# Attention's product buffers, the early parts and the wo blocks of a gated scan kernel: four moves in the order of work

## The chip, the cores and the metric

The kernel runs on one core of one Trainium2 chip. The metric is the device time of one execution in microseconds (us). Before the change it is 760.67 us, the median of three runs (758.78 to 761.59).

Engines are named as in the profile: PE is TensorE, DVE VectorE, ACT ScalarE, POOL GpSimd, SP SyncE. SP computes nothing here and issues most of the DMA transfers, one behind the other. Each engine works through its own instructions in the order of the program and waits for other engines through semaphores.

## The reference

`x` is 2048 rows of 640 numbers. It is normalised by rows (`xn`), goes through attention and through a gated layer, and the two are multiplied:

```
xn = layernorm(x)
s  = attention(xn @ wqkv) @ wo        # 32 heads of 20; each row looks at 8 earlier rows, two apart
g  = silu(((xn @ w_gate) * (xn @ w_up)) @ w_down)
out = x + s * g
```

All arrays are float32.

## The kernel before

**Numbers in two parts.** The matmuls take their operands as float32r. The kernel splits every operand in a high part (a copy in that type, made by ACT) and a low part (the rest, a subtraction by DVE or POOL), and each product is three products: high by high, high by low, low by high. `split` (line 107) and `mm3` (line 114) do this.

**Rows.** The 2048 rows are 16 tiles of 128, four to a chunk. Tile 0 to 7 are the even rows, 8 to 15 the odd ones. Tiles come in by DMA, `moments_q` (320) takes mean and variance on DVE, `scales` (327) makes the factors from them: a square root on ACT, a sum and a reciprocal on DVE, and for tiles 8 to 15 the rest, seven small steps, on POOL. `spread` (337) brings the factors to all partitions with one small matmul and an ACT copy, `apply_q` (349) applies them on ACT, `trans_q` (359) turns a tile on DVE and splits it. The result is `xT`, four chunks.

**Products with fewer multiplications.** The gate and up products, the product with w_down and the one with wo are done as a seven product scheme on two by two blocks (Strassen's), which needs sums and differences of blocks of both operands. For chunks 0 and 1 those of `xT` are made early: `early_sums(k)` (583), eight additions and subtractions on POOL, and `early_high(k)` (596), which splits four results on POOL and stores the eight parts with eight DMAs on SP, to `t_scr` and `e_scr`. k is 0 or 1. The results live in the memory of two earlier tiles, `xc` (tag "kv") and `xe` (tag "t"). For chunks 2 and 3 the same is done later by `differences` (1187) on ACT and POOL.

**Buffers.** Memory is handed out by tags: `st(shape, "t", 2)` is one of two buffers of the tag "t". A tile gets a buffer that is free once everything that used it before is done; the waits follow from that. At the start the two "t" buffers are `xa` (at the end tiles 12 to 14) and `xe`. `attention` takes both: `twice` (line 466) for the products of queries and keys, and `terms` (467) for those of weights and values. After attention the "t" buffers take the rows of wo. The tag "gh" has five buffers for pieces of the gate and up results.

**Order of work.** The order is written out by hand, and `attention` is a generator that the rest drives: `advance(budget)` (608) lets it issue instructions worth so much time after each piece of PE work. Attention works in 12 units of four or six heads. In each unit DVE does a product of queries and keys (line 527) and its sum (534) for each pair of the eight positions; a unit later DVE forms weights times values (498), and POOL (in the last unit partly DVE) adds them up (504). The keys and values of a unit come back from DRAM, where `qkv` (420) has stored them by a DMA on ACT's queue (445).

The start of the program, around the change (lines 1105 to 1160), goes: qkv of tiles 4 and 5, three steps of `early_sums(0)`, `scales(8)`, the other five steps, qkv of tiles 6 and 7, moments of tiles 12 to 15, `scales(12)`, `early_high(0)`, `early_sums(1)`, `early_high(1)`, `gate_up(0, 1)` with `spread(8)` in its middle, trans_q of tiles 8 to 10, `gate_up(1, 1)` with `spread(12)` in its middle, qkv of tiles 8 to 11, `gate_up(0, 2)`, the last trans_q, and then attention begins beside qkv of tiles 12 to 15. `gate_up(f, ch)` (627) is one block of gate and up columns for one chunk. Its last multiplication (653) and the store of h (657) are put off to the next `finish_piece()`.

**The groups.** From block f = 2 on, `group(f, c0)` (1284) does a block of columns for two chunks in seven products, at the steps n = 0 to 6. The middle blocks (3 to 10) are done for chunks 2 and 3 (`second` = 0) and then for chunks 0 and 1 (`second` = 1). `hold` (1292) has ACT copy a product into a gh buffer, `gate_a` (1305), `gate_b` (1295), `up_a` (1308) add or multiply on DVE, `up_b` (1298) and `h_b` (1301) on POOL or DVE. up_a and h_b are followed by stores of h (1281) and are put off to step 0 of the next group. The dictionary `beside` hangs further work on a step: the key (f, second, n) is the place. f0 is 10, f1 is 11, the last block.

**The product with wo.** `load_wo` (685) loads rows of wo, `split_wo` (692) splits one, `sums_wo` (930) forms four differences on DVE (936 to 939). `load_pair(p)` (967) loads two tiles of attention's result, `turn_pair(p)` (976) turns them on DVE and forms their sums, `begin_last` (1430) finishes attention and issues the loads of wo. Before the change these hang on the steps as follows:

```
beside.update({(f0, 1, 0): lambda: begin_last(), (f0, 1, 4): lambda: split_wo(0, nc.vector),
               (f0, 1, 5): lambda: split_wo(1, nc.vector), (f0, 1, 6): lambda: sums_wo()})
```

Inside `begin_last`, `load_pair(0)` follows the loads of wo. `load_pair(1)` hangs on (f1, 0, 0) and `turn_pair(0)` on (f1, 0, 1).

Later come the product with wo in pairs of tiles, and the product with w_down with the gate and the sum with x, which fill PE to the end.

Of the kernel before, what the change touches and what calls it, by code (L numbers as in the profile page):

```python
# [19 lines left out]
P = 128  # L20
# [4 lines left out]
NE = NT // DIL  # L25
# [9 lines left out]
CMAX = max(GROUPS) * DH  # L35
# [21 lines left out]
def kernel(  # L57
# [11 lines left out]
    nc = tc.nc  # L69
# [11 lines left out]
    def st(shape, tag, bufs, dt=F32):  # L81
        cnt[0] += 1
        return sb.tile(shape, dt, tag=tag, bufs=bufs, name=f"{tag}_{cnt[0]}")
# [214 lines left out]
    def low_parts(n=None):  # L298
        for _ in range(len(halves) if n is None else n):
            halves.pop(0)()  # L300
# [23 lines left out]
    def load_xq(s, n, t):  # L324
        nc.sync.dma_start(t, xq[:, s - TPC:s - TPC + n, :])

    def scales(s0):
        mv, mr = stat[s0]
        eng = nc.vector if s0 == TPC else nc.gpsimd
        rstd(mv[:, :, 1], mr[:, 1, :], TPC, eng=eng)  # L330
        eng.tensor_scalar(mr[:, 0, :], mv[:, :, 0], -1.0, None, op0=ALU.mult)
        eng.tensor_mul(mr[:, 0, :], mr[:, 0, :], mr[:, 1, :])
        own[s0] = part(few[:, s0 // TPC % 2 * 32:], [P, NQ, 2, TPC])
        eng.tensor_mul(own[s0], mr.unsqueeze(1).to_broadcast([P, NQ, 2, TPC]),
                             quarter.unsqueeze(2).unsqueeze(3).to_broadcast([P, NQ, 2, TPC]))

    def spread(s0):

        p = pt([P, NQ, 2, TPC], "q", 3)
        nc.tensor.matmul(p, sel, own[s0], start=True, stop=True)  # L340
        spread_t[s0] = part(few[:, 64 + s0 // TPC % 2 * 32:], [P, NQ, 2, TPC])
        nc.scalar.activation(spread_t[s0], p, AF.Copy)
        apply_q(s0)
# [117 lines left out]
    def attention():  # L461

        def flat(y):
            return y.rearrange("p i c -> p (i c)")

        twice = st([P, 2, NE * CMAX], "t", 2)
        terms = st([P, 2, NE * CMAX], "t", 2)
        spots = NE * W
        m_ps = weights[0:1, CH - spots:].rearrange("p (i w) -> p i w", w=W)
        nc.vector.tensor_copy(m_ps, mask)  # L470
# [125 lines left out]
    def early_high(k):  # L596

        r0, r1, a, b = early_t[:4]
        for n, (j, y) in enumerate((("T1", a), ("T2", b), ("T3", r0), ("T4", r1))):
            hi = early_t[4 + n].bitcast(F32R)  # L600
            nc.gpsimd.tensor_copy(hi, y)
            nc.gpsimd.tensor_sub(y.bitcast(F32R), y, hi.bitcast(F32))
            for l, t in enumerate((early_t[4 + n], y)):
                nc.sync.dma_start(t_scr[:, T2_UNIT[j, l] + k] if j != "T4" else e_scr[l][:, k], t)
# [22 lines left out]
    def gate_up(f, ch, between=(), amid=(), part=None, early=()):  # L627
        if part is None:
            pp = [pt([P, CH], "g", 2), pt([P, CH], "u", 2)]
            c = slice(0, CH)  # L630
        else:
            pp, c = part, slice(CH // 2, CH)
        last = (f, ch) == (KF - 1, NCH - 1)
        if early:
            gate_up_half(f, ch, 0, pp[0], c, parts=ALL3[:1], last=False)
            for act in early:
                act()
        gate_up_half(f, ch, 0, pp[0], c, parts=ALL3[1:] if early else ALL3, first=not early)
        for act in amid:
            act()  # L640
        gs = st([P, CH], "gh", 5)
        nc.scalar.activation(gs, pp[0], AF.Copy)
        for act in between:
            act()
        share = (c.stop - c.start) / CH
        finish_piece()
        advance(PACE * 3.25 * share)
        gate_up_half(f, ch, 1, pp[1], c)

        def finish():  # L650
            hs = st([P, CH], "gh", 5)
            if not last:
                nc.vector.tensor_mul(hs, pp[1], gs)
            else:
                nc.scalar.activation(hs, pp[1], AF.Copy)
                nc.gpsimd.tensor_mul(hs, hs, gs)
            nc.sync.dma_start(h_scr[ch * TPC:(ch + 1) * TPC, :, f, :].rearrange("t p c -> p t c"),
                              hs.rearrange("p (t c) -> p t c", c=P))

        unfinished.append(finish)  # L660
        if last:
            finish_piece()
        advance(PACE * 3.25 * share)
# [28 lines left out]
    def split_wo(k, eng=nc.gpsimd):  # L692
        y = slot([P, 2, D])
        hi, lo = y[:, 0], y[:, 1]
        split(eng, wo_raw.pop(k), hi, lo)
        wo_s[k] = hi, lo
# [233 lines left out]
    def sums_wo():  # L930

        r, u = wo_keep[:2]
        b11, b12, b21, b22 = r[:, :, :HALF], r[:, :, HALF:], u[:, :, :HALF], u[:, :, HALF:]
        t1, t2, t3 = (wo_sum[0][:, 2 * i:2 * i + 2] for i in range(3))
        t4 = st([P, KS, HALF], "o", 1)
        nc.vector.tensor_sub(t1, b12, b11)
        nc.vector.tensor_sub(t3, b22, b12)
        nc.vector.tensor_sub(t2, b22, t1)
        nc.vector.tensor_sub(t4, b21, t2)
        wo_keep.append({"T1": t1, "T3": t3, "T2": t2, "T4": t4})  # L940
# [26 lines left out]
    def load_pair(p):  # L967
        t = slot([P, 2, D], F32) if p == 2 else st([P, 2 if p else 5, D], "t" if p else "kv", 2)
        if not p:
            wo_sum.append(t[:, 2:].rearrange("p a (b c) -> p (a b) c", c=HALF))  # L970
            t = t[:, :2]
        load_o(2 * p, 2, t)
        t = t.rearrange("p a c -> p (a c)")
        pair_raw[p] = t[:, :3 * KS * P].rearrange("p (a c) -> p a c", c=P)
# [35 lines left out]
    def lo_pair(p, part):  # L1010
        z, raw = pair_z[p, part]
        nc.vector.tensor_sub(z[1], raw, z[0].bitcast(F32))
# [94 lines left out]
    early = early_sums(0)  # L1107
# [4 lines left out]
    load_xq(8, 2, xp)  # L1112
    load_xq(10, 2, xs)
    scales(8)
    for _ in early:
        pass
    qkv(0, 0, 6)
    qkv(0, 0, 7)
    moments_q(12, 4)
    load_xq(12, 3, xa)  # L1120
    load_xq(15, 1, xd)
    scales(12)
    early_high(0)
    for _ in early_sums(1):
        pass
    early_high(1)
    gate_up(0, 1, amid=(lambda: spread(8),))
    nc.scalar.activation(st([P, 1], "exp", 1), eps_t, AF.Exp)
    trans_q(8)
    trans_q(9)  # L1130
# [15 lines left out]
    gate_up(0, 2)  # L1146
    trans_q(15)
    low_parts()
    for a in range(2):
        nc.sync.dma_start(e_scr[2 + a], xT[3][a][:, 0:2, :].bitcast(F32))  # L1150
    made.add(0)
# [9 lines left out]
    f0, f1 = KF - 2, KF - 1  # L1161
# [234 lines left out]
    for m, t in ((m, t) for m in range(1, len(MADE)) for t in range(DIL)):  # L1396
# [23 lines left out]
        elif (m, r) == (last, 1):  # L1420
            for k in range(2):
# [2 lines left out]
    w_split(2, "R")  # L1424
    w_sum.pop(2)
    load_wf(3)
    beside.update({(f0, 1, 0): lambda: begin_last(), (f0, 1, 4): lambda: split_wo(0, nc.vector),
                   (f0, 1, 5): lambda: split_wo(1, nc.vector), (f0, 1, 6): lambda: sums_wo()})

    def begin_last():  # L1430
        advance(1e9)
        wo_keep.extend([load_wo((0, 1)), load_wo((2, 3)), load_wo((4,))[:, 0]])
        load_pair(0)
        begin_wd("T4")

    wo_keep = []
# [15 lines left out]
    for f in range(2, f1):  # L1452
# [18 lines left out]
        if f == F_TWO:  # L1471
# [1 line left out]
        group(f, 2)  # L1473
        group(f, 0, 1)
    places.clear()
    beside.update({(f1, 0, 0): lambda: load_pair(1), (f1, 0, 1): lambda: turn_pair(0), (f1, 0, 4): lambda: (hi_pair(0, 0), lo_pair(0, 0)),
                   (f1, 0, 6): lambda: (hi_pair(0, 1), lo_pair(0, 1), load_e(3, 1, 3)), (f1, 0, 5): sum_w5,
                   (f1, 0, 3): lambda: load_e(3, 0, 2)})
    group(f1)
# [192 lines left out]
```

## Time and profile before

| | |
|---|---|
| runs | 760.67 us median (758.78 to 761.59) |
| the profiled execution | 757.63 us |
| its span in the trace | 755.9 us |
| PE busy | 740.4 us (98%) |
| DVE busy | 612.5 us (81%) |
| POOL busy | 464.2 us (61%) |
| ACT busy | 301.4 us (40%) |
| DMA | 132.98 MB, 176 GB/s on average |

A row of the timeline gives the start in us from the span's start, the duration, the engine, the line of the kernel, the operation, what it writes and reads by the program's names, the shapes, and how many like it are merged in the row. In brackets stands how long the engine was idle ahead of it, and who ended that idle time. A row of waits gives the waiting engine with its tile and line, the one waited for, and then the sum in us, how many times, and the longest. "SPq" and "ACTq" mark the issue of a DMA. PEld is the loading of weights into PE. In a table by stages each row has the stretch, the busy time of PE, PEld, DVE, ACT and POOL, the granted PE clock as a share of full speed, the share of DMA, and GB/s.

### The profile page before, as it was taken

How to read it: one execution, taken by the hardware profiler on the slowest of the kernel's cores; microseconds unless marked ns; L12 is line 12 of the kernel's file. 1: busy time of each engine (PE TensorE's matmuls, PEld its weight loads, DVE VectorE, ACT ScalarE, POOL GpSimd, SP SyncE). 2: the span in 40 equal slices, each digit the busy share in tenths (PEclk: the TensorE clock that was granted, in tenths of full speed). 3: DMA queues.
4: the chain of work that ended last, by engine and by line, in shares of the span. 5: the costliest groups of instructions: out<-in, count | busy, mean ns of one | idle time of the engine just before them, and what ended most of it. 6: DMA issues, size and time to landing. Idle time of an engine off the chain costs nothing. (4 is left out here: it accounts for less than half of the span.)

```text
span 755.9 us, 11101 instructions
## 1 busy us (share of the span) xinstructions
PE 740.4 (98%) x4054; PEld 673.8 (89%) x4054; DVE 612.5 (81%) x720; ACT 301.4 (40%) x577; POOL 464.2 (61%) x389
## 2 busy tenths in 40 slices
PE   8999999899999999999999999998999999999997
PEld 6988879888899998888887888886999999999997
DVE  7666499599978778999899899667898787777775
ACT  5648222323233233233233323333465664444442
POOL 6169636978789779978888989876749900000000
PEclk9999999999999999999999999999999999999999
DMA  8464583586454638776246433366568565555534
GB/s 326 155 194 156 175 278 121 174 264 193 137 170 143 204 131 262 219 204 208 89 123 169 117 90 87 94 176 178 154 178 239 190 254 189 188 188 189 189 105 140
DMA packets 103493, 132.98 MB, mean 176 GB/s; under 512 B 22696, under 2 KB 74404, under 8 KB 103438
## 3 DMA queue, kind: packets, MB, share of 16 engines
q1 hardware_dynamic: 84686, 112.77, 48.0%
q10 hardware_dynamic: 17600, 14.26, 5.8%
q0 software_dynamic: 1152, 5.24, 2.1%
q8 instruction: 32, 0.52, 0.3%
q14 instruction: 23, 0.19, 0.1%
HBM read 83.58 MB, written 47.81 MB: 174 GB/s over the span
## 5 line engine op out<-in xcount | busy, mean ns | idle before, releaser
L504 POOL TENSOR_TENSOR o<-o,t 128x960 f32<-128x960 f32 (+1 forms) x69 | 139.7, 2025 | 19.1 <-DVE t L498 17.6
L498 DVE TENSOR_TENSOR t<-e,kv 128x960 f32<-128x960 f32 (+1 forms) x96 | 99.4, 1037 | 22.1 <-POOL o L504 22.0
L527 DVE TENSOR_TENSOR t<-q,kv 128x1920 f32<-128x1920 f32 (+1 forms) x48 | 92.4, 1925 | 11.4 <-DMA e_scr<-t 8.0
L534 DVE TENSOR_REDUCE lg<-t 128x96 f32<-128x1920 f32 (+1 forms) x48 | 92.2, 1921 | 0.1
L428 PE MATMUL q<-s,xc 128*128 128x360 f32 (+1 forms) x450 | 85.3, 340 | 2.7 <-ACT s L441 2.0
L110 POOL TENSOR_TENSOR s<-wraw,s 128x384 fp32r<-128x384 f32 (+6 forms) x58 | 70.1, 1219 | 28.8 <-ACT s L109 27.0
L428 PEld LDWEIGHTS q<-s,xc 128*128 128x128 f32 x450 | 76.9, 191 | 7.0 <-ACT s L441 2.3
L1292 ACT ACTIVATE gh<-g 128x512 f32<-128x512 f32 x54 | 32.3, 598 | 117.9 <-PE g L1325 105.0
L428 PE MATMUL u<-s,xc 128*128 128x360 f32 (+1 forms) x360 | 66.6, 336 | 0.0
L428 PEld LDWEIGHTS u<-s,xc 128*128 128x128 f32 x360 | 61.0, 188 | 2.3
L428 PE MATMUL g<-s,xc 128*128 128x360 f32 (+1 forms) x330 | 62.3, 340 | 0.0
L428 PEld LDWEIGHTS g<-s,xc 128*128 128x128 f32 x330 | 56.6, 188 | 2.6
L896 PE MATMUL q<-xc,s 128*128 128x320 f32 x342 | 55.5, 309 | 0.0
L1325 PE MATMUL u<-xc,s 128*128 128x512 f32 x216 | 55.1, 390 | 0.0
L1325 PE MATMUL g<-s,s 128*128 128x512 f32 x216 | 54.8, 389 | 0.0
L896 PEld LDWEIGHTS q<-xc,s 128*128 128x128 f32 x342 | 51.5, 188 | 0.0
L1325 PEld LDWEIGHTS u<-xc,s 128*128 128x128 f32 x216 | 40.4, 188 | 8.9 <-ACT gh L1292 0.6
L1325 PEld LDWEIGHTS g<-s,s 128*128 128x128 f32 x216 | 40.5, 188 | 8.4
L109 ACT ACTIVATE s<-wraw 128x384 fp32r<-128x384 f32 (+6 forms) x59 | 33.5, 587 | 29.9 <-PE g L1325 9.4
L504 POOL TENSOR_TENSOR o<-t 128x960 f32<-128x960 f32 (+1 forms) x12 | 24.4, 2033 | 34.0 <-DVE t L498 24.9
L1325 PE MATMUL g<-xc,s 128*128 128x512 f32 x168 | 42.3, 396 | 2.9 <-ACT gh L1292 2.9
L119 PE MATMUL u<-xc,s 128*128 128x512 f32 (+1 forms) x180 | 40.4, 375 | 1.8 <-ACT pk L441 0.9
(367 smaller groups left out, 1568.4 us busy)
## 6 DMA issues: line engine op xcount, KB each, us to landing
h_scr<-gh SPq DMA_DIRECT2D x48, 256.0 KB, 2.5
wraw<-in_wgu SPq DMA_DIRECT2D x11, 640.0 KB, 4.4
kv<-qkv_scr SPq DMA_DIRECT2D x14, 480.0 KB, 5.5
qkv_scr<-s ACTq DMA_DIRECT2D x18, 360.0 KB, 3.0
t<-h_scr SPq DMA_DIRECT2D x8, 768.0 KB, 7.6
kv<-qkv_scr SPq DMA_DIRECT2D x14, 367.5 KB, 6.2
s_scr<-gh SPq DMA_DIRECT2D x16, 320.0 KB, 4.3
gh<-s_scr SPq DMA_DIRECT2D x16, 320.0 KB, 3.3
```

Of the source, the lines that this page charges most:

```text
L109: nc.scalar.activation(hi, raw, AF.Copy)
L110: eng.tensor_sub(lo, raw, hi.bitcast(F32))
L119: nc.tensor.matmul(acc, a, b, start=first and n == 0, stop=last and n == len(runs) - 1)
L428: nc.tensor.matmul(p, xT[(r * NE + i) // TPC][a][:, k, t0:t0 + P], wq[m][b][k], start=n == 0, stop=n == len(runs) - 1, skip_group_check=ac ...
L498: nc.vector.tensor_mul(t.rearrange("p (n d) -> p n d", d=DH), e[:, :, w].unsqueeze(2).to_broadcast([P, NE * nh, DH]), v)
L504: return NE * c * cost, lambda: eng.tensor_add(y, z, t)
L527: nc.vector.tensor_mul(t, q, k)
L534: nc.vector.tensor_reduce(out=lg[:, :, j:j + 2].rearrange("p n a -> p a n"), in_=t.rearrange("p a (n d) -> p a n d", d=DH), op=ALU.add, ax ...
L896: nc.tensor.matmul(p, y[:, i, k], wd_t[name][k][:, l], start=new and r == 0, stop=r == len(runs) - 1, skip_group_check=True)
L1292: nc.scalar.activation(kept[j], b["ACACABA"[j]], AF.Copy)
L1325: nc.tensor.matmul(y, w, x, start=j in (0, 1, 5) and r == 0, stop=r == len(runs) - 1, skip_group_check=True)
```

## The change

Four moves; no instruction is added or taken away.

1. In `attention`, the lines that make `twice` and `terms` change places.
2. At the start, `gate_up(0, 1)` with `spread(8)` comes before `scales(12)`; three more steps of `early_sums(0)` stay where they were, and the last two come behind `scales(12)`.
3. `early_high(1)` moves from behind `early_sums(1)` to behind the last `trans_q` and its low parts.
4. The loads of wo (`begin_last`) go from (f0, 1, 0) to (f0, 0, 5); `load_pair(0)` leaves `begin_last` and comes with `sums_wo` at (f0, 1, 1); the two splits go to (f0, 1, 2) and (f0, 1, 3); `turn_pair(0)` joins `load_pair(1)` at (f1, 0, 0), ahead of it.

```diff
@@ attention
+        terms = st([P, 2, NE * CMAX], "t", 2)
         twice = st([P, 2, NE * CMAX], "t", 2)
-        terms = st([P, 2, NE * CMAX], "t", 2)
@@ the start
     scales(8)
-    for _ in early:
-        pass
+    for _ in range(3):
+        next(early)
     qkv(0, 0, 6)
     qkv(0, 0, 7)
     moments_q(12, 4)
     load_xq(12, 3, xa)
     load_xq(15, 1, xd)
+    gate_up(0, 1, amid=(lambda: spread(8),))
     scales(12)
+    for _ in early:
+        pass
     early_high(0)
     for _ in early_sums(1):
         pass
-    early_high(1)
-    gate_up(0, 1, amid=(lambda: spread(8),))
     nc.scalar.activation(st([P, 1], "exp", 1), eps_t, AF.Exp)
...
     trans_q(15)
     low_parts()
+    early_high(1)
     for a in range(2):
         nc.sync.dma_start(e_scr[2 + a], xT[3][a][:, 0:2, :].bitcast(F32))
@@ the last groups
-    beside.update({(f0, 1, 0): lambda: begin_last(), (f0, 1, 4): lambda: split_wo(0, nc.vector),
-                   (f0, 1, 5): lambda: split_wo(1, nc.vector), (f0, 1, 6): lambda: sums_wo()})
+    beside.update({(f0, 0, 5): lambda: begin_last(), (f0, 1, 1): lambda: (load_pair(0), sums_wo()),
+                   (f0, 1, 2): lambda: split_wo(0, nc.vector), (f0, 1, 3): lambda: split_wo(1, nc.vector)})
 
     def begin_last():
         advance(1e9)
         wo_keep.extend([load_wo((0, 1)), load_wo((2, 3)), load_wo((4,))[:, 0]])
-        load_pair(0)
         begin_wd("T4")
...
-    beside.update({(f1, 0, 0): lambda: load_pair(1), (f1, 0, 1): lambda: turn_pair(0), (f1, 0, 4): lambda: (hi_pair(0, 0), lo_pair(0, 0)),
+    beside.update({(f1, 0, 0): lambda: (turn_pair(0), load_pair(1)), (f1, 0, 4): lambda: (hi_pair(0, 0), lo_pair(0, 0)),
```

## The prediction

> **What bounds the kernel now.** First the page's head: how long, and which engine is full.
>
> ```profile
> span 755.9 us, 11101 instructions
> PE 740.4 (98%) x4054; PEld 673.8 (89%) x4054; DVE 612.5 (81%) x720; ACT 301.4 (40%) x577; POOL 464.2 (61%) x389
> ```
>
> TensorE (PE) is busy 98% of the span. The matmuls themselves are not touched by the change, so it can win only what PE loses: 15.5 us of idle time (755.9 less 740.4), and matmuls that run at a low clock. So I next asked the waits of PE alone, and the table of 5 us stretches for the granted clock (the column after the five engines).
>
> ```profile
> PE g L1325 <- ACT gh L1292: 2.9, 2, 2.4
> PE q L428 <- ACT s L441: 2.0, 1, 2.0
> ```
>
> ```profile
> 140.00:145.00 5.00, 3.53 (x14) 3.53 (x15) 3.19 (x5) 2.61 (x6) 5.00 (x4) 0.73 0.69 206
> 520.00:525.00 5.00, 5.00 (x16) 3.92 (x16) 4.61 (x6) 3.08 (x5) 3.70 (x4) 0.66 0.70 186
> ```
>
> The reader is to see two things: PE stands still in few places, and behind the two longest gaps the granted clock falls to 0.73 and 0.66, so a gap costs more than its length. Then I read the timeline at each gap, to find who was late.
>
> **Part 1: the spread of tiles 12 to 15.** The timeline from 49 to 58 us:
>
> ```profile
> 49.24 1.29 POOL L593 TENSOR_TENSOR kv<-kv,xc 128x512 f32<-128x512 f32 x1
> ...
> 51.37 0.30 ACT L263 ACTIVATE lg<-mvo,eps 128x4 f32<-128x4 f32 x1 [3.40 <-DVE mvo L256]
> ...
> 53.22 1.30 POOL L593 TENSOR_TENSOR kv<-xc,kv 128x512 f32<-128x512 f32 x1
> ...
> 57.73 0.41 PE L340 MATMUL q<-lg,lg 128*128 128x32 f32 x2 [1.08 <-POOL lg L334]
> ```
>
> PE's second spread matmul (L340) waits 1.08 us for GpSimd's (POOL's) last step of scales(12). POOL works through five steps of early_sums(0) (L593) before it. After the change three stand before it and two behind: 2 x 1.30 = 2.6 us earlier, more than the 1.08. The price: the square root of scales(12) on ScalarE (ACT, L263) now stands behind spread(8)'s copy (L342), four scalings and one eviction. ACT waited 3.40 us for the moments there, so the copy moves up into that wait, and I put the root at about 52.5, before POOL is through its third step at 53.1. If that cover were gone, POOL would wait, us for us. Worth **1.08 us**. POOL's total work and the end of its early steps stay where they are.
>
> **Part 2: the late half of the early parts, and the two product buffers.** early_high(1) is four casts and four subtractions on POOL and eight stores on the DMA queue of SyncE (SP). On POOL nothing is queued between its old and its new place, so its times there stay. On SP it is moved past two h stores and the two loads of wqkv block 1, which no longer stand behind it; the stores e_scr 2 and 3 stay behind it. Nothing reads the stored parts until the groups, so their own lateness costs nothing. The order of PE's instructions is the same. Now the timeline from 81 to 100 us:
>
> ```profile
> 81.70 0.97 ACT L488 ACTIVATE q<-q 128x960 f32<-128x960 f32 x1
> ...
> 87.08 0.33 SPq L604 DMA_DIRECT2D e_scr<-t  x1
> ...
> 90.49 0.52 ACTq L445 DMA_DIRECT2D qkv_scr<-s  x1
> 90.59 2.16 DVE L527 TENSOR_TENSOR t<-q,kv 128x1920 f32<-128x1920 f32 x1 [8.01 <-DMA e_scr<-t]
> ...
> 91.11 0.47 ACT L441 ACTIVATE pk<-g 128x360 f32<-128x360 f32 x1 [7.74 <-PE g L119]
> ...
> 92.00 3.69 PE L119 MATMUL u<-xc,s 128*128 128x512 f32 x15 [0.93 <-ACT pk L441]
> ...
> 99.23 0.68 DVE L653 TENSOR_TENSOR gh<-u,gh 128x512 f32<-128x512 f32 x1
> ...
> 99.97 3.72 PE L119 MATMUL u<-xc,s 128*128 128x512 f32 x15 [0.88 <-DVE gh L653]
> ...
> 100.99 0.32 SPq L408 DMA_DIRECT2D q<-qkv_scr  x1
> ```
>
> Attention's first product (L527, into the buffer called twice) has its query by 82.67 (81.70 + 0.97), but VectorE (DVE) waits 8.01 us for the store e_scr<-t. That store reads xe, the second of the two "t" buffers: so twice lies in xe, which early_high(1) held last. Before, xe comes free first in the program (early_high(1) precedes trans_q(14), the last reader of xa), and the buffer that is used first (twice; terms is first written a unit later) got the one that is free first. After, trans_q(14) precedes early_high(1): xa is free first. I take it that twice, still used first, gets xa, whichever of the two lines stands first, and attention starts at about 82.7 instead of 90.59: 7.9 us earlier. That is the step where I choose; if the order of the lines decided, twice would stay in xe (a rival below). The store of ACT at 90.49 is issued in the same moment as the wait ends: it hangs on one of these stores too, and blocks the eviction at 91.11. With SP's order changed I expect it to hang on an earlier one, by about 86.
>
> Queued behind L527 on DVE is L653, which frees PE's bank: 99.23 becomes about 91.3. Both PE waits (0.93 and 0.88) go: **1.81 us**. Attention's next unit needs its keys; their loads (L408 at 100.99) stand on SP behind L657, the store of L653's result, which moves with it, and behind POOL's clearing of the buffer, which follows early_high(1) and the splitting of block 1, whose load no longer waits for SP. I let them move along; what they come late by, DVE loses again. PE is then 1.08 + 1.81 = 2.9 us earlier at 110 us, DVE 7.9.
>
> Next gap, from 134 to 153 us:
>
> ```profile
> 119.31 2.26 POOL L504 TENSOR_TENSOR o<-t 128x960 f32<-128x960 f32 x1 [17.01 <-DVE t L498]
> ...
> 134.54 2.56 PE L428 MATMUL g<-s,xc 128*128 128x360 f32 x15
> ...
> 136.94 2.56 PE L428 MATMUL u<-s,xc 128*128 128x360 f32 x15
> ...
> 138.51 0.63 ACT L1197 ACTIVATE s<-gh 128x512 fp32r<-128x512 f32 x1 [7.15 <-POOL gh L1193]
> ...
> 141.47 4.21 PE L428 MATMUL q<-s,xc 128*128 128x360 f32 x15 [1.97 <-ACT s L441]
> ...
> 153.00 3.43 PE L428 MATMUL g<-s,xc 128*128 128x480 f32 x15
> ```
>
> ACT waits 7.15 us for POOL's differences, and the evictions behind it hold PE. POOL had itself begun late: it stood 17.01 us for attention's first values on DVE. With DVE 7.9 us earlier and PE 2.9, ACT's wait shrinks by 5.0 to about 2; earlier waits of 7.15 at this rhythm just sufficed to stop PE, so 2 doesn't. The gap's whole cost: blocks of 15 follow each other at 2.40 us (136.94 behind 134.54); from 136.94 to 153.00 are five of them, 16.06 us instead of 12.0. Worth **4.06 us**: 1.97 idle, the rest low clock. What is late next: nothing that stops PE until 404 us.
>
> [...]
>
> **Part 3: wo sooner.** The timeline of the last two groups of products:
>
> ```profile
> 496.97 0.36 SPq L575 DMA_DIRECT2D o_scr<-o  x1
> ...
> 499.25 2.07 SPq L688 DMA_DIRECT2D t<-in_wo  x4
> ...
> 505.15 3.51 DVE L110 TENSOR_TENSOR s<-t,s 128x640 fp32r<-128x640 f32 x2 [5.85 <-ACT s L109]
> ...
> 507.04 1.52 PE L1325 MATMUL g<-xc,pk 128*128 128x512 f32 x6
> ...
> 508.40 2.20 PE L1325 MATMUL q<-xc,pk 128*128 128x512 f32 x9
> ...
> 509.18 1.31 DVE L936 TENSOR_TENSOR kv<-t 128x640 f32<-128x640 f32 x1
> ...
> 514.52 0.83 DVE L939 TENSOR_TENSOR o<-t,kv 128x640 f32<-128x640 f32 x1
> ...
> 515.20 2.20 PE L1325 MATMUL u<-xc,s 128*128 128x512 f32 x9
> 515.26 0.68 DVE L1308 TENSOR_TENSOR gh<-gh,g 128x512 f32<-128x512 f32 x1
> ...
> 519.13 0.60 ACT L1292 ACTIVATE gh<-g 128x512 f32<-128x512 f32 x1 [4.43 <-DVE wraw L985]
> ...
> 519.78 3.04 PE L1325 MATMUL g<-xc,s 128*128 128x512 f32 x9 [2.38 <-ACT gh L1292]
> ...
> 526.99 3.56 PE L119 MATMUL g<-xc,s 128*128 128x512 f32 x15
> ```
>
> ```profile
> DMA to landing us min/median/max: 3.8/5.0/6.1
> ```
>
> (The last is the answer for tile in_wo.) DVE does split_wo(0) and (1), then four subtractions of sums_wo (509.18 to 515.35, 6.2 us), and only then L1308, whose store gives back a gh buffer. ACT's eviction (L1292) waits for that buffer, and PE for ACT. At full clock six matmuls take 1.36 us (508.40 less 507.04), 0.227 each. From 515.20 to 526.99 stand 9, 9 and 15 of them, 33 x 0.227 = 7.48 us, but 11.79 passed. The gap costs **4.31 us**.
>
> After, the five wo loads stand right behind the o store: 497.35 instead of 499.25, because SP still waits for attention's last add. Two h stores go behind them, some 2 us later. The subtractions now stand one step behind the group's start, in the time in which DVE idled 5.85 us, so L1308 of the last group moves from 515.26 to about 511.4 and its buffer is back in time. turn_pair(0) is one step earlier but in the same place among DVE's instructions; load_pair(1) is behind it in the text alone, on another queue. The new wait: the first subtraction waits for its rows, and behind it stand L1305 of this group, both splits and L1308. L1305 frees the bank that PE's block at 508.40 writes. Fourth row issued at 498.9, landed after 3.8 to 6.1; then from three subtractions at 0.83 (L939; the first one needs earlier rows) to all four in 6.2; then L1305, taken like L1308 at 0.68: free between 505.9 and 511.9. PE loses 0 to 3.5 us, and up to 1.9 more at low clock (4.31 less 2.38). With the median landing and three subtractions at 1.5 it is free at 509.0, so I take **0.5 us** lost.
>
> **Sum**: 1.08 + 1.81 + 4.06 + 4.31 - 0.50 = 10.8 us. The profiled execution took 757.63 us, its span 755.9, with 1.7 around it: it would be 746.9. The runs before have a median of 760.67, 3.0 above the profiled one; on that footing the change gives **749.9 us**. DVE is then ahead by about as much as PE (7.9 against 7.0 us at 153), so I expect nothing to eat the gain between the two places.
>
> **The rivals.**
> A: the first product keeps xe, and the buffers don't change places in fact. Then DVE starts at 90.6, L653 at 99.23 holds PE as before, and the gap at 139.5 comes back. Left is 4.31 - 0.5 = 3.8: 756.9. For it: the text gives terms first. Against: the present row shows that the first one used got the first one free.
> B: the rows of wo land late or a gh buffer is not back when ACT wants it (the h stores go 2 us later). The gap of 4.31 is then exchanged for one of the same size: 760.67 - 6.95 = 753.7. For it: 6.1 us is the longest landing. Against: the median.
> C: the clock falls at 140 and 520 us for another reason than the gaps, and stays low. Idle time alone comes back: 1.08 + 1.81 + 1.97 + 2.38 - 0.5 = 6.7, so 753.9. Against: the two rows of clock. [...]
> D, slower: the ring of five gh buffers. They are handed on in the order in which they come free, and part 2 deals that order anew. If ACT then gets in each half of a group the one whose store is still in flight, PE loses each time what it loses today once:
>
> ```profile
> 404.09 2.20 PE L1325 MATMUL u<-xc,s 128*128 128x512 f32 x9
> ...
> 409.01 1.53 PE L1325 MATMUL g<-xc,pk 128*128 128x512 f32 x6
> ```
>
> Between the two rows stand 18 matmuls (9 of them left out), 4.08 us at 0.227; 4.92 passed, 0.84 lost. Groups 3 to 10 have 16 halves; 15 new ones cost 12.6, and with B's exchange only 6.95 stands against it: 760.67 + 5.6 = 766.3. It is slower than before by over 0.5% from 13 halves on. Against: it happens once now.
>
> **How the numbers follow.** Forecast 0.66, A 0.10, B 0.13, C 0.02, D 0.09. The forecast's own range is 746.5 (no stall in part 3 and a level nearer the profiled run) to 752.5 (half of the bound there); about one case in ten of it may fall outside, so to hold 8 in 10 the range must reach past B and C to A: 746.0 to 757.5. Over 0.5% (3.8 us, about what a measurement of this kernel can tell from no change) is below 756.9: forecast, B, C and a part of A, 0.83; A's rest, 0.08, is the same; D, 0.09, slower.
>
> **What would show it.** L527 of unit 0 begins near 82.7 with no wait for e_scr<-t; PE's rows at L119 near 90 and 98 carry no wait; L1197's second wait is below 4 us and the clock stays 1.00 from 135 to 155; the spread at 56.7 has no wait; L1308 of the last group lies near 504 on the new time axis and PE's gap of 2.38 is gone. A wait of L527 for e_scr<-t (A), a wait of PE at the q block for L1305 or at n6 for L1292 (B), slow matmuls without a gap before them (C), or L1292 waiting for h_scr<-gh in most groups (D) would make it wrong.

## The result, and the profile after

After the change the kernel takes 751.43 us (median of 4 runs, 749.97 to 752.84), before it 760.58 us beside them (4 runs): a ratio of 0.988, with a 95% interval of 0.9855 to 0.9909. The forecast was 749.9 us. The traces show that two of its three parts came as forecast or better, that the third turned into a loss, and that a gain of 2.1 us and a loss of 2.2 us came which no step had named. The profiled execution of after took 751.81 us, the one of before 757.63: they differ by 5.8 us, the medians by 9.15. In the sums below the traces are set beside each other, so they add up to 5.9 us of span.

The head of after's page, and the waits of PE with their total, number and longest:

```profile
span 750.0 us, 11103 instructions
PE 737.2 (98%) x4054; PEld 670.5 (89%) x4054; DVE 610.2 (81%) x720; ACT 302.1 (40%) x577; POOL 463.9 (62%) x389
```

```profile
PE g L1327 <- ACT gh L1294: 3.9, 3, 2.9
PE q L224 <- POOL lg masks.py:199: 1.4, 1, 1.4
PE e L340 <- POOL lg L334: 1.0, 1, 1.0
```

ACT's evictions with a wait for a buffer (L1294, L1292 before; in the later part after's lines are two higher) still stand at the top, with 3.9 us for 2.9. The wait of 2.0 for ACT's evictions (L441) is gone.

**Part 1.** The timeline of after from 49 to 58 us: ACT's root of scales(12) and PE's second spread matmul.

```profile
51.94 0.28 ACT L263 ACTIVATE lg<-mvo,eps 128x4 f32<-128x4 f32 x1
...
56.25 0.30 PE L340 MATMUL q<-lg,lg 128*128 128x32 f32 x2
```

Neither carries a wait any more; the root stands at 51.94 (52.5 was forecast), behind the copy, and costs nothing.

**Part 2.** The timeline from 78 to 98 us, then PE's rows alone:

```profile
80.48 2.13 DVE L527 TENSOR_TENSOR t<-q,kv 128x1920 f32<-128x1920 f32 x1
...
85.05 0.52 ACTq L445 DMA_DIRECT2D qkv_scr<-s  x1
85.67 0.47 ACT L441 ACTIVATE pk<-g 128x360 f32<-128x360 f32 x1 [3.88 <-DMA t_scr<-t]
```

```profile
89.32 3.56 PE L119 MATMUL u<-xc,s 128*128 128x512 f32 x15
...
96.12 3.56 PE L119 MATMUL u<-xc,s 128*128 128x512 f32 x15
```

Attention's first product starts at 80.48 instead of 90.59 and waits for nothing. ACT's store is issued at 85.05; it hangs on an earlier store (t_scr), as forecast. Both of PE's waits are gone. ACT's wait for POOL's differences, the second one of 7.15 us before, is shorter, but not as short as forecast (about 2):

```profile
128.45 0.63 ACT L1199 ACTIVATE s<-gh 128x512 fp32r<-128x512 f32 x1 [4.65 <-POOL gh L1195]
```

Then the place of the gap near 140, in the timeline of PE and in the table of 5 us stretches (granted clock behind the five engines):

```profile
137.52 2.56 PE L428 MATMUL g<-s,xc 128*128 128x360 f32 x15
139.92 2.56 PE L428 MATMUL u<-s,xc 128*128 128x360 f32 x15
142.32 2.56 PE L428 MATMUL q<-s,xc 128*128 128x360 f32 x15
144.72 3.41 PE L428 MATMUL g<-s,xc 128*128 128x480 f32 x15
```

```profile
140.00:145.00 5.00, 5.00 (x33) 4.97 (x32) 2.94 (x2) 1.39 (x4) 3.71 (x4) 1.00 1.11 289
```

Blocks follow at 2.40 us through the old gap, and the clock stays at 1.00 (0.73 before).

**Something not forecast.** Here is the projection much later, before and after, in the timeline of PE from 205 to 216 us. Both clocks are 1.00 and no row has a wait:

```profile
207.49 2.63 PE L428 MATMUL q<-s,xc 128*128 128x360 f32 x15
209.96 2.63 PE L428 MATMUL g<-s,xc 128*128 128x360 f32 x15
```

```profile
206.32 2.56 PE L428 MATMUL q<-s,xc 128*128 128x360 f32 x15
208.72 2.56 PE L428 MATMUL g<-s,xc 128*128 128x360 f32 x15
```

The same blocks follow at 2.47 us before and at 2.40 after. That is 4.5 ns in each matmul; over the 32 blocks between 205 and 284 us it makes 2.1 us.

**Part 3.** The timeline from 484 to 512 us: columns are start, length, engine and line; "SPq" is the issue of a DMA.

```profile
489.15 2.62 SPq L688 DMA_DIRECT2D t<-in_wo  x4
...
492.35 1.17 SPq L1283 DMA_DIRECT2D h_scr<-gh  x2
...
494.27 0.83 DVE L936 TENSOR_TENSOR kv<-t 128x640 f32<-128x640 f32 x1 [3.80 <-DMA t<-in_wo]
494.74 2.21 PE L1327 MATMUL u<-xc,s 128*128 128x512 f32 x9
497.65 0.82 DVE L937 TENSOR_TENSOR kv<-t,t 128x640 f32<-128x640 f32 x1 [2.56 <-DMA t<-in_wo]
...
499.25 0.60 ACT L1294 ACTIVATE gh<-g 128x512 f32<-128x512 f32 x1 [4.15 <-DMA h_scr<-gh]
...
499.90 4.21 PE L1327 MATMUL g<-xc,s 128*128 128x512 f32 x9 [2.95 <-ACT gh L1294]
503.90 2.54 PE L1327 MATMUL g<-xc,pk 128*128 128x512 f32 x6
...
506.28 2.24 PE L1327 MATMUL q<-xc,pk 128*128 128x512 f32 x9
508.36 1.52 PE L1327 MATMUL g<-s,s 128*128 128x512 f32 x6
```

SP issues the loads of wo first, then the two h stores. The eviction at 499.25 waits for the first of the two h stores to give its gh buffer back: issued at 492.35, it landed 6.8 us later, just ahead of the eviction. In before, where the same stores stand ahead of the loads, they landed 2.8 and 3.3 us after their issue. PE stops for 2.95 us, and the nine matmuls behind the stop take 4.21 us. From 494.74 to 508.36 pass 13.62 us for 33 matmuls, which take 33 x 0.227 = 7.48 at full pace: **6.1 us lost**. The old gap is gone (515.16, 517.20 and 520.60 are the starts there, without a wait).

Since PE's 4,054 matmuls have the same order in both kernels, the start of each one in before less its start in after shows where the time went:

| place (time of before) | forecast, us | measured, us |
|---|---|---|
| spread of tiles 12 to 15, 57.7 | 1.08 | 1.33 |
| two waits near 92 and 100 | 1.81 | 2.63 |
| gap at 139.5 and the clock behind it | 4.06 | 4.08 |
| pace of the 360-wide blocks, 205 to 284 | 0 | 2.13 |
| groups, 284 to 436 | 0 | -2.20 |
| old gap in the last groups | 4.31 | 4.30 |
| new gap in the last groups | -0.50 | -6.14 |
| pairs of the wo product, 530 to 550 | 0 | -0.51 |

With 0.25 at the very start the measured column makes 5.9 us, the forecast's 10.8.

### The profile page after: what moved, and what is told of

It reads as the page before. It is cut to its first block, busy times and chain, and to the rows that moved or that the text cites. A ratio compares the mean times of both kernels' runs of the same rounds, so it can differ in the third digit from the quotient of the medians.

```text
span 750.0 us, 11103 instructions
## 1 busy us (share of the span) xinstructions
PE 737.2 (98%) x4054; PEld 670.5 (89%) x4054; DVE 610.2 (81%) x720; ACT 302.1 (40%) x577; POOL 463.9 (62%) x389
## 4 chain that ended last, share of the span: by engine, by line
PE 84%; POOL 4%; DVE 4%; DMA 3%; ACT 2%; issue 2%; SPq 1%; POOLq 0%; ACTq 0%; DVEq 0%
PE g L1327 11%; PE q L428 9%; PE q L896 8%; PE u L428 8%; PE g L428 8%; PE u L1327 7%; PE u L896 6%; PE g L119 4%; PE u L119 4%; PE q L1327 3%; PE g L896 3%; PE e L896 3%; PE q L119 2%; DMA h_scr<-gh 2%; POOL o L504 2%
## 5 line engine op out<-in xcount | busy, mean ns | idle before, releaser
L527 DVE TENSOR_TENSOR t<-q,kv 128x1920 f32<-128x1920 f32 (+1 forms) x48 | 92.4, 1926 | 5.3 <-DMA kv<-qkv_scr 5.2
L428 PE MATMUL q<-s,xc 128*128 128x360 f32 (+1 forms) x450 | 82.7, 334 | 0.6 <-DVE lg L266 0.5
L1294 ACT ACTIVATE gh<-g 128x512 f32<-128x512 f32 x54 | 32.3, 598 | 122.3 <-PE g L1327 104.8
L428 PEld LDWEIGHTS q<-s,xc 128*128 128x128 f32 x450 | 74.9, 188 | 4.5 <-DVE lg L266 0.7
L109 ACT ACTIVATE s<-wraw 128x384 fp32r<-128x384 f32 (+6 forms) x59 | 33.2, 586 | 28.7 <-PE g L1327 9.0
L1327 PEld LDWEIGHTS g<-xc,s 128*128 128x128 f32 x168 | 32.4, 195 | 12.2 <-ACT gh L1294 5.5
```

The costliest lines, as they stand in the source:

```text
L109: nc.scalar.activation(hi, raw, AF.Copy)
L428: nc.tensor.matmul(p, xT[(r * NE + i) // TPC][a][:, k, t0:t0 + P], wq[m][b][k], start=n == 0, stop=n == len(runs) - 1, skip_group_check=ac ...
L527: nc.vector.tensor_mul(t, q, k)
L1294: nc.scalar.activation(kept[j], b["ACACABA"[j]], AF.Copy)
L1327: nc.tensor.matmul(y, w, x, start=j in (0, 1, 5) and r == 0, stop=r == len(runs) - 1, skip_group_check=True)
```

## The experiments

Times of each table row are beside the kernel before on the same chip (medians of 758.4 to 760.2 us; one run of it beside pe_stop). PE's lead is by how much it starts a matmul earlier than the same one starts in the profiled execution of before.

| kernel | time, us | ratio, 95% | span, us |
|---|---|---|---|
| start_only | 749.18 | 0.9867 to 0.9893 | 746.7 |
| wo_only | 760.76 | 1.0017 to 1.0039 | 759.2 |
| loads_behind | 751.58 | 0.9896 to 0.9924 | 751.9 |
| sums_first | 748.94 | 0.9865 to 0.9890 | 747.6 |
| terms_first | 761.36 | 1.0018 to 1.0048 | 762.0 |
| spread_only | 753.29 | 0.9918 to 0.9944 | 751.6 |
| late_half_only | 750.77 | 0.9855 to 0.9895 | 750.1 |
| lines_back | 749.70 | 0.9843 to 0.9894 | 747.3 |
| turn_later | 747.90 | 0.9845 to 0.9880 | 746.0 |
| after_again | 750.76 | 0.9884 to 0.9912 | 749.4 |
| act_held, one run | 750.34 | not given | 748.6 |
| pe_stop, one run | 757.59 | not given | 755.8 |

The theory after reading the trace (T): the start (parts 1 and 2) brings the whole gain, and wo's move costs, because its loads stand before the h stores on SP.

**start_only and wo_only: the two halves.** The first is after with the wo part as it was, the second before with the wo part alone.

```diff
-    beside.update({(f0, 0, 5): lambda: begin_last(), (f0, 1, 1): lambda: (load_pair(0), sums_wo()),
-                   (f0, 1, 2): lambda: split_wo(0, nc.vector), (f0, 1, 3): lambda: split_wo(1, nc.vector)})
+    beside.update({(f0, 1, 0): lambda: begin_last(), (f0, 1, 4): lambda: split_wo(0, nc.vector),
+                   (f0, 1, 5): lambda: split_wo(1, nc.vector), (f0, 1, 6): lambda: sums_wo()})
```

> Moves 1 to 3 without move 4 (wo as before). Theory T: the start is worth 1.08 + 1.81 + 4.06 = 6.95 us on the trace, and move 4 loses 1.8 us again, so this kernel is faster than the changed one: span about 748.9 against 755.9 before, with the gap of some 2.4 us at the last groups back. Rival R: the start is worth only the 5.9 us by which the spans differ and move 4 is neutral; then the span is about 750.0.

> Move 4 alone. Theory T: the two h stores stand behind five wo loads on SP, a gh buffer comes back late, and the last groups lose 6.1 us where they lost 4.3: 1.8 us slower than before (span about 757.7), with ACT's hold waiting for h_scr<-gh. Rival R: neutral, span 755.9, since the gap has only changed its place.

start_only's span is 746.7, 2.2 below what T gave; wo_only is slower than before, by 0.3% in the ratio. Its row at the place, in ACT's timeline:

```profile
509.02 0.60 ACT L1292 ACTIVATE gh<-g 128x512 f32<-128x512 f32 x1 [3.77 <-DMA h_scr<-gh]
```

The same eviction waits for the same store without any of the other moves. So the gain is the start's, and the third part by itself is a small loss. T was too low on wo_only: a span of 757.7 was expected, 759.2 came.

**loads_behind: only the order on SP.** The loads of wo stand behind the two h stores, with the rest as in after:

```diff
-    beside.update({(f0, 0, 5): lambda: begin_last(), (f0, 1, 1): lambda: (load_pair(0), sums_wo()),
+    beside.update({(f0, 1, 0): lambda: begin_last(), (f0, 1, 1): lambda: (load_pair(0), sums_wo()),
```

> The changed kernel with the loads of wo put back to (f0, 1, 0), behind the h stores; the rest of move 4 stays. Theory T (the h stores' place on SP is the cause): ACT's wait of 4.2 us for h_scr<-gh and PE's gap of 2.95 us at the last product of the group go; the rows of wo come some 2 us later, so DVE's subtractions end later and PE may wait 1 to 3 us at the q block for L1307. Span 746 to 749. Rival R2 (the rows of wo, for which DVE waits 3.8 and 2.6 us, are the cause): later rows make it worse, the span is 751 or more.

```profile
496.11 0.74 ACT L109 ACTIVATE s<-t 128x640 fp32r<-128x640 f32 x1 [2.13 <-DMA t<-in_wo]
...
497.39 2.37 PE L1327 MATMUL u<-xc,s 128*128 128x512 f32 x9 [1.27 <-ACT gh L1294]
...
505.82 3.75 PE L1327 MATMUL q<-xc,pk 128*128 128x512 f32 x9 [2.65 <-DVE gh L1307]
```

The wait for the store is gone, as T says, but the time isn't back. The rows of wo now land later (DVE's first difference starts at 497.24 us, in after at 494.27), the four differences hold DVE longer (to 505.16 us, in after to 500.13), and behind them stands the sum (L1307) that frees the bank of PE's block q. This is the new wait that the prediction had priced at 0.5 us; here it is 2.65 and a slow block behind it (3.75 us for nine matmuls). The 1.27 us at 497.39 is one more: that eviction stands on ACT behind a copy of split_wo (L109), which waited 2.13 us for a row of wo. T's span of 746 to 749 was missed. The 751.9 is what R2 gave, and R2 is right that late rows cost time; but ACT's wait for the store went with the order on SP, as T said. So there are two waits at this place, and each place of the loads trades one for the other.

**sums_first: the differences early, the splits late.** The loads as in loads_behind, the differences at the step at which the rows are there, and the two splits only in the next group, in which after's DVE idles for 4.00 us:

```diff
+    beside.update({(f0, 1, 0): lambda: begin_last(), (f0, 1, 5): lambda: sums_wo()})
...
+    beside.update({(f1, 0, 0): lambda: (split_wo(0, nc.vector), split_wo(1, nc.vector), load_pair(1)), (f1, 0, 2): lambda: turn_pair(0), (f1, 0, 4): lambda: (hi_pair(0, 0), lo_pair(0, 0)),
```

> The start of the changed kernel; wo loaded as before the change at (f0, 1, 0); the differences sums_wo at (f0, 1, 5); both splits behind them at (f1, 0, 0), behind the put off multiplication; turn_pair(0) at (f1, 0, 2). Theory T: up_a of the last half is no longer behind the splits and its store is in time, no gap in the last groups: span 755.9 - 6.95 - 4.3 = about 744.7. Rival R2 (rows of wo too late): DVE stands before the first subtraction, gate_b and up_a come late, PE's gap stays at 2 us or more: span 748 to 750.

PE runs through the last groups without a stop: its lead is 7.8 us at 436 and 12.1 at 530. Then it drops to 8.2, at a place where before had no wait; DVE's rows there and PE's:

```profile
526.96 1.56 DVE L710 STREAM_TRANSPOSE s<-s 128x640 f32<-128x640 f32 x2
...
531.72 1.05 DVE L800 TENSOR_TENSOR lg<-wraw,lg 128x320 f32<-128x320 f32 x1
...
532.69 1.47 DVE L1012 TENSOR_TENSOR xc<-s,xc 128x640 fp32r<-128x640 f32 x1
```

```profile
PE e L1033 <- DVE xc L1012: 1.8, 1, 1.8
```

DVE is now the late one: the pair's low part (L1012) stands behind the transposes of a later pair (L710). The gap in the last groups was really worth its 4.3 us, but DVE was full behind it (without a wait from 518.55 to 537.77 us).

**turn_later and after_again.** sums_first with those transposes one place later, beside after unchanged, on one chip:

```diff
     g3 = gate(f1, 3)
-    turn_pair(2)
     up(f1, 3, g3)
...
         if p == 0:
+            turn_pair(2)
             load_pair(4)
```

> sums_first with the transposes and sums of the third pair of attention's rows (3.5 us on VectorE) moved from ahead of the last tile's product to behind the first pair's sixth product. T (VectorE's queue made PE wait 1.8 us for the second pair's low part): that wait is gone and with it the low clock behind it, span 747.6 - 2.6 = 745.0, time near 746.5. Rival R (VectorE is full from 519 to 537, so the work only moves the wait): a wait of 1 to 2 us for the third pair's low part opens near 545, span 747 to 748.

> The kernel after unchanged, beside the others on one chip. Expected 750 to 753 us, and its ratio to before 0.986 to 0.991; if the wo part costs what the traces say, it stands 2 to 3.5 us above start_only's ratio of 0.988 read on its own chip, which would be 747 to 749.

turn_later takes 747.90 us, after 750.76 beside it; their intervals don't touch. The wait of 1.8 is gone from its list of PE's waits, and the longest of what is left there is:

```profile
PE g L1327 <- ACT gh L1294: 1.6, 2, 1.3
```

T's 746.5 was 1.4 too low: PE still drops 1.9 us of its lead between 550 and 600. It has the lowest median of this study, 0.4% below after. That it beats start_only, which leaves wo where it was, is not shown: the two ran on different chips, and their ratios (0.9845 to 0.9880 and 0.9867 to 0.9893) overlap.

**terms_first: twice in the other buffer.** One write to `terms` ahead of the first use of `twice` hands out the two buffers the other way round; the rest is after:

```diff
         terms = st([P, 2, NE * CMAX], "t", 2)
         twice = st([P, 2, NE * CMAX], "t", 2)
+        nc.vector.memset(terms[:, 0, 0:1], 0.0)
```

> The kernel after, but `terms` is touched ahead of `twice`, so that `twice` gets the later of the two product buffers again, as in the kernel before; the second early parts stay late and wo stays as in after. Theory T (the buffer is what frees attention's start): the product's wait for the store to e_scr is back, L527 starts near 89.3 us (90.59 of before less the 1.25 of part 1), PE's waits of 0.93 and 0.88 near 90 and 98 are back, and so is the gap near 139 with its 4.06 us and the 0.07 us per block of 15 afterwards (2.467 against 2.400 us, 34 blocks, 2.2 us): the span is 750.0 + 1.8 + 4.1 + 2.2 = 758.1 us. Rival R (moving the second early parts is what frees it, the buffer adds little): L527 starts before 84, no gap near 139, span within 1 us of 750.0.

```profile
91.81 2.16 DVE L528 TENSOR_TENSOR t<-q,kv 128x1920 f32<-128x1920 f32 x1 [11.23 <-DMA e_scr<-t]
...
101.19 6.58 PE L119 MATMUL u<-xc,s 128*128 128x512 f32 x15 [4.89 <-DVE gh L654]
```

The wait for e_scr is back, and longer than before's 8.01, since the late early parts give the buffer back later. The time is 761.36, slower than before. So the buffer, not the later instructions as such, frees attention's start; rival R is out. T's 758.1 was 3.9 us low in the span, and its sum came out otherwise: PE's wait of 4.89 put the kernel 8.1 us behind after at 110 us, where T had 1.8, while the place near 139 cost it 1.5 us against after, where T had 4.06.

**lines_back: the two lines alone.** After, with `twice` and `terms` written in their old order:

```diff
-        terms = st([P, 2, NE * CMAX], "t", 2)
         twice = st([P, 2, NE * CMAX], "t", 2)
+        terms = st([P, 2, NE * CMAX], "t", 2)
```

> The kernel after with the two lines that take the product buffers in their old order. T (a buffer goes to whoever first writes it, not to the line that names it first): the same kernel, 751 us within 0.3%, span 749 to 751. Rival R (the order of the two lines decides): terms_first's 761 us.

749.70 us, and L527 starts at 80.15: nothing changes. The first of the four moves does nothing beside the others; which buffer `twice` gets follows from the moves at the start.

**spread_only and late_half_only: moves 2 and 3, one at a time, on before.**

```diff
# spread_only
-    for _ in early:
-        pass
+    for _ in range(3):
+        next(early)
...
+    gate_up(0, 1, amid=(lambda: spread(8),))
     scales(12)
+    for _ in early:
+        pass
...
-    gate_up(0, 1, amid=(lambda: spread(8),))
# late_half_only
-    early_high(1)
...
     low_parts()
+    early_high(1)
```

> The kernel before with its tiles' deviations and the rest of the early sums in after's order, the second early parts still early, wo as in before. T: part 1 is there (the spread of tiles 12 to 15 without its wait, 1.1 us), and `twice` has the free buffer, but the second early parts' four loads and sums stay ahead of attention, so L527 starts between 82.7 and 88 us; no gap of over 1 us near 139 and a pitch of 2.400 us of the 360-wide blocks from 200 to 270: span 747 to 751 (start_only's 746.7 and up to 4 more). Rival R: the late second early parts carry most of the gain, the gap near 139 and the pitch of 2.467 stay: span 754 to 755.

> The kernel before with the second early parts moved behind the low parts, and nothing else (`twice` gets the free buffer by this as well). T: all of part 2 is there without part 1: L527 starts 1.1 us later than in start_only, near 81.6, no PE waits near 90 and 98, no gap near 139 and a pitch of 2.400 us: span start_only's 746.7 + 1.1 = 747.8 or a little more, time near 750. Rival R (the deviations' place is needed, since scales and the early sums stand ahead of the product on VectorE): L527 after 84, a wait of 0.5 to 2 us near 90, span 750 to 752.

spread_only, in its timeline around 90 us:

```profile
80.37 2.13 DVE L527 TENSOR_TENSOR t<-q,kv 128x1920 f32<-128x1920 f32 x1
...
90.37 0.47 ACT L441 ACTIVATE pk<-g 128x360 f32<-128x360 f32 x1 [8.59 <-DMA e_scr<-t]
...
91.25 5.32 PE L119 MATMUL u<-xc,s 128*128 128x512 f32 x15 [1.78 <-ACT pk L441]
```

Attention starts at 80.37 here too, but ACT's store still hangs on a late e_scr store, its eviction waits 8.59 us, and PE stops for 1.78 us, with 5.32 us for the block behind it instead of 3.56 (after's row at 89.32). late_half_only has L527 at 81.53, no wait at 90 and 98, and only part 1's wait left. Its lead at 284 us is 9.25, start_only's 10.92. spread_only's lead is 6.74. So either move alone gives `twice` the free buffer and removes the gap near 140, with a pitch of 2.400 us in both, as T had it; the late early parts add the order on SP that ACT's store hangs on. Their spans are 0.6 and 2.3 us above what T gave (747 to 751, and 747.8); late_half_only loses 3.7 us in the groups, where start_only loses 2.3. One thing here is against the prediction: in spread_only `early_high(1)` still stands ahead of `trans_q(14)`, so the buffer of xe has its last user first, as in before, and yet `twice` didn't wait for it.

**act_held and pe_stop: what sets the slower pace?** In before, wo_only and terms_first, blocks of 360 follow at 2.467 us late in the projection; in all the others at 2.400. Two things go with that: a stop among the 360-wide blocks, and `twice` in the later buffer. These two kernels were to stop PE while `twice` lies as in after.

```diff
# act_held, in the loop over tiles 4 to 7 of the second unit
+        if i == 10:
+            for _ in range(48):
+                nc.scalar.activation(hold_act, eps_t, AF.Copy)
# pe_stop, ahead of qkv(m, r, i)
+            if (m, r, i) == (1, 1, 5):
+                for k in (0, 0, 1, 1):
+                    y = xT[(r * NE + i) // TPC][0][:, k, i % TPC * P:(i % TPC + 1) * P]
+                    nc.scalar.activation(y, y.bitcast(F32), AF.Copy, scale=-1.0)
```

> The kernel after with 48 copies of one column (each at most 0.20 us, as the one-column exponential took) in ScalarE's queue ahead of the eleventh tile's projection of the second unit, so that PE finds no free bank and stops for 1 to 4 us among the 360-wide blocks, where after has no gap; `twice` stays in the free buffer. Theory S (a stop among 360-wide blocks sets the slower pace that before has from 145 to 284 us): after the stop the blocks of 15 follow at 2.467 us up to 274, 34 or so of them, 2.2 us lost beside the stop. Rival P (the pace goes with where `twice` lies: before, wo_only and terms_first have it in one buffer, the kernels with 2.400 us in the other): after the stop the blocks still follow at 2.400 us.

> The kernel after with four extra ScalarE operations of 128 columns each ahead of one 360-wide block of 15 near 137.5 us: they turn the sign of two 128x128 pieces of that block's input and turn it back, so that PE can't start the block until ScalarE has read the block before and done them. PE stops for 1.2 to 3 us among the 360-wide blocks; act_held had meant to do that, but its condition was never met, since the loop that it sat in has 8 tiles, so it ran the kernel after. `twice` stays in the free buffer. Theory S (a stop among 360-wide blocks sets the slower pace that before has from 145 to 284 us): after the stop the blocks of 15 follow at 2.467 us up to 270, 34 of them with those right behind the stop, 2.2 us lost beside the stop, span 749.4 + 2.2 + the stop of 2 = 753.6. Rival P (the pace goes with where `twice` lies): after the stop the blocks still follow at 2.400 us, span 751.4.

In act_held the condition is never met, since that loop ends at tile 7: it is after once more, and says nothing on the pace. pe_stop does stop PE. Its timelines at the stop and 65 us later:

```profile
141.06 4.53 PE L428 MATMUL g<-s,xc 128*128 128x360 f32 x15 [3.58 <-ACT xc L1415]
145.42 2.63 PE L428 MATMUL u<-s,xc 128*128 128x360 f32 x15
...
209.78 2.63 PE L428 MATMUL u<-s,xc 128*128 128x360 f32 x15
212.24 2.63 PE L428 MATMUL q<-s,xc 128*128 128x360 f32 x15
```

Behind the block that follows the stop, all 34 blocks of 360 columns come at 2.467 us, up to the last near 279 us, with 480-wide blocks in between; before the stop they came at 2.400. Theory S holds and P falls, in this one run. pe_stop's span is 755.8, after_again's 749.4.

## Why the prediction was right, and where it was wrong

The time was near (751.4 for 749.9), for reasons that are right in two parts of three, and in part by luck: the step that failed is part 3, and what it lost was made up by a gain that no step had named (2.13 us) and by which execution of before had been profiled (below).

- **Part 1** was right: 1.33 us for 1.08.
- **Part 2** was right in its outcome: the order of the two lines doesn't matter (lines_back), who writes first does (terms_first), and L527 starts without a wait. The rule behind it, that the first used gets the buffer whose last user stands first in the program, falls with spread_only; what decides instead stays open. The two PE waits were mis-sized: 2.63 us for 1.81. Rows of 3.56 us follow each other at 3.40, so each row overlaps the next by 0.16 us, and the idle column leaves that out at each stop; the blocks behind the waits were longer too (3.69 and 3.72 us in the rows quoted in the prediction, 3.56 after), and so was one at 107.01 us, by 0.2, ahead of which no idle time is shown.
- **The gap at 139.5** was right in its size: 4.08 us for 4.06. ACT's wait, which was to shrink to about 2 us and in any case below 4, still was 4.65; that was short enough for PE not to stop. The step left out what stays behind the gap: the pace of the later blocks, 2.13 us, which pe_stop shows to come from such a stop.
- **Part 3** failed. The step said that the buffer of L1308 "is back in time" and charged only the sum behind DVE's differences, at 0.5 us. That much was as forecast: L1308 (L1310 in after) stands at 504.35 where "near 504" was said, and the old gap is gone. But the step asked for no other buffer. What came is the second half of rival B: the h stores that "go behind them, some 2 us later" belong to the half of the group before, and exactly these held the gh buffer. They were issued 2.5 us later, near what the prediction had, but behind the loads they took 6.8 us to land instead of some 3, so the first was back 6.5 us later (499.16, where before's landing of 500.87 would be 492.64 with PE's lead of 8.23 us taken off). The wait that was charged, PE's at the q block, did not come at all (506.28, without a wait). The prediction had the cause in its own text, priced as a rival of the same size as the old gap (4.31), and gave it 0.13. It cost 6.1 us for 4.3 gained. wo_only shows that the move alone does not pay; loads_behind that the charged wait is real as well, when the rows come later (2.65 us).
- **"I expect nothing to eat the gain between the two places"** failed too, by 2.2 us between 284 and 436. In three places PE stops where before it did not. The first stop, 0.41 us at 322.52, is behind an eviction that waits for an h store; the second, 0.34 us at 333.35, behind one that waits for POOL's step of the gate (L1303); in the third PE itself waits for POOL's split of weights. The rows of ACT for the first two and of PE for the third:

```profile
321.87 0.60 ACT L1294 ACTIVATE gh<-g 128x512 f32<-128x512 f32 x1 [2.52 <-DMA h_scr<-gh]
...
332.70 0.60 ACT L1294 ACTIVATE gh<-u 128x512 f32<-128x512 f32 x1 [2.37 <-POOL gh L1303]
```

```profile
406.71 0.50 PE L1327 MATMUL u<-xc,s 128*128 128x512 f32 x1 [0.25 <-POOL s L110]
```

Only the first is rival D's mechanism, in one place and not in sixteen; the other two hang on POOL. The same first stop stands in start_only (1.59 us) and after_again (1.76), behind the same wait. No run took any of them away, so the cause is read from the traces only.

Gains 3.5 us above the forecast stand against 8.4 us of losses beyond it, or 10.8 less 4.9, the 5.9 of the traces. That the medians differ by 9.15 is a matter of which executions were profiled: after's was the longest of four profiled runs of that kernel (spans of 750.0, 749.4, 748.6 and 747.3, with after_again, act_held and lines_back, which ran the same instructions), before's was 3 us below its median, which is most of it.

## What to carry to other kernels

Before moving loads forward on a queue, list what stands behind them on that queue, and ask of each store which buffer it gives back and who wants it next; here that cost 3.3 to 6.1 us, in four executions of the same instructions. Which of two buffers a tile gets can hang on moves far from the lines that name it; read it from the waits in the trace, not from the text. And a stop of PE cost three things here: its length (1.97 us in before at 139.5), often the clock behind it (0.73 there), and among the 360-wide blocks the pace long after (2.467 us for 15 matmuls instead of 2.400); count from the pitch of equal blocks, not from the idle column.

## What the runs showed of the hardware

**The clock behind a gap differed from one execution to the next.** Four executions of the same instructions (after, after_again, act_held, lines_back) had a gap at the same place: 2.95, 2.40, 2.50 and 2.81 us. The stretch of 2.5 us behind it, in after and in lines_back:

```profile
500.00:502.50 2.50, 2.50 (x6) 2.02 (x7) 2.50 (x4) 1.61 (x3) 1.85 (x1) 0.50 0.63 126
```

```profile
500.00:502.50 2.50, 2.34 (x10) 1.96 (x11) 2.50 (x4) 1.89 (x4) 1.58 (x1) 1.00 0.68 140
```

The granted clock was 0.50 in one and 1.00 in the other, and the nine matmuls behind the gap took 4.21 and 2.33 us. In after_again and act_held the clock was 0.73 and 0.66 there. The loss at this place was 6.1, 4.5, 4.6 and 3.3 us. So what such a gap costs in one trace, like the 4.31 us in before, is not a constant, and the spans of these four executions differ by up to 2.7 us. Their loss in the groups differs too: 2.2, 3.5, 2.3 and 2.7 us. The length of the gap does not order them: the longer gap of 2.81 us (lines_back) left the clock at 1.00, behind the shorter one of 2.40 (after_again) it was 0.73. In before it was 0.73 from 140 to 145 us, behind a gap of 1.97, and 0.66 from 520 to 525, behind one of 2.38; one of 1.78 in spread_only was followed by a block of 5.32 us instead of 3.56. What decides whether the clock falls was not shown.

**A stop among the 360-wide blocks left a slower pace.** It was 2.467 instead of 2.400 us for 15 matmuls, at a granted clock of 1.00, for some 135 us after pe_stop's stop of 3.58 us, after before's of 1.97 and after a third of 1.10 us in terms_first, behind which the clock stayed at 1.00:

```profile
148.03 2.56 PE L428 MATMUL u<-s,xc 128*128 128x360 f32 x15
151.70 2.74 PE L428 MATMUL q<-s,xc 128*128 128x360 f32 x15 [1.10 <-ACT s L441]
```

Its 360-wide blocks after 206 us came at 2.467 us too. Stops ahead of 512-wide blocks (4.89 us in terms_first, 1.78 in spread_only) left the next 360-wide blocks at 2.400. What keeps the pace, and what would bring it back, stays open.
